# First batch of an attention and MLP kernel stacked on 128 partitions, with fp32 products in column tiles, on one Trainium2 core

## Chip, cores and metric

The kernel runs on one core of a Trainium2 chip. The metric is device time in microseconds (us). Three runs of the kernel before took 362.1, 361.82 and 361.71 us; the median is 361.82.

A core has these engines, named as the profile names them: PE (TensorE, matrix products; PEld are its weight loads), DVE (VectorE), ACT (ScalarE), POOL (GpSimd) and SP (only issues transfers). Each has an instruction queue of its own and takes it in order. Transfers (DMAs) are issued by SP, ACT or POOL and run on 16 shared DMA engines; only those issued by POOL convert the data type on the way. Products land in PSUM, eight banks of 128 partitions x 512 fp32 values.

## Reference

```python
kv  = einsum('bhsd,bhse->bhde', k, v)              # b = 8, h = 8, s = 576, d = 64
out = einsum('bhsd,bhde->bhse', q, kv)
x   = out / sqrt(mean(out*out, -1) + 1e-6) * g_norm    # heads side by side: [8, 576, 512]
a1  = alpha1 * x + beta1
tok = einsum('ts,bsd->btd', w_tok, a1)             # w_tok 576 x 576
u   = x + lam * tok
a2  = alpha2 * u + beta2
out = u + lam * (relu(a2 @ w_ch1) @ w_ch2)         # 512 -> 2048 -> 512
```

All inputs and the output are fp32.

## The kernel before

The eight batches run one after the other. For each there are two parts. The first, of small "fill" products, makes kv = k^T v per head, turns q so that d lies on the partitions, multiplies both, norms the result (`norm_ops`) and mixes tokens with W_tok (`tok`), which gives u in `xm`; then u is scaled and turned into `a2m`. The second part, the "main" stream, is the two big products: ch1 (L1020, 16 blocks of 4 products of 512 columns, then relu on ACT) and ch2 (L1049). The tokens 512 to 575 of two batches share a tail tile.

Nothing is issued in the order in which it is written. `P.op`, `P.dma` and `P.mm` only record operations with a cost, and `schedule()` plays them through: each engine takes the first operation of its list that is ready by the planner's clock, and PE weaves fills between the main products. Before the main stream begins, PE is given idlers (L558, a bf16 product of ones) wherever nothing is ready, and one idler between the products of a slow fill. `P.shift`, a table by operation number, moves single operations in the lists. The order found so is emitted as fixed instruction lists with semaphore waits.

The prologue, all that comes before the main stream, handles batch 0 in four pairs of heads, p = 0 to 3:
- SP loads k, q and v of each pair (`load_early` and L587) on 96 partitions, six tokens each (rows of 1536 bytes), and after the second pair the matrix W_tok, in fp32 (L592, L594).
- k is rounded to fp32r (a shortened fp32 for PE) by POOL (`round_early`, L682), v by ACT (L1144) or POOL (L1148).
- POOL copies q (L693), PE transposes it 96x96 in fp32 (L699), ACT copies it to `qt` (`qt_early`).
- `kv_early` makes k^T v of a pair as six 128x128 fp32r products (L736), of which DVE and ACT keep the two 64x64 blocks on the diagonal (`kvc`).
- `norm_pair` (L868) and `norm_tail` (L887) multiply qt by kvc; per 512 columns `norm_ops` needs ACT (square), DVE (reduce), ACT (root), DVE (reciprocal, scale, multiply to `rm`), then ACT copies x out and POOL multiplies it by g (L839, L841).
- `wt_group` transposes W_tok in fp32 on PE (L1099, L1102), ACT writes it as bf16 to `wt`; `wsums` (L1121, L1123) adds its columns.
- The rows alpha1 lam g and beta1 lam are computed on one partition by DVE, in ten steps, and spread by PE in three bf16 parts (`e1_rows`, L662).
- `tok_pair` mixes the tokens of one pair (L933, 80 products of 128 columns in all), DVE adds (L941), `a2_pair` transposes u (L972) and ACT scales it to `a2m` (L976).

PSUM tiles of the prologue come from banks 1 to 7.

Batch 1 uses the same early path: k and q by SP in fp32 on 96 partitions, k rounded by DVE (L685), v by a casting load on POOL. Batch 2 takes k and v by casting loads (`load_kv`, `kv`, L760 and L766) but its q still by the early path: SP, POOL copy, PE transposes L699. From batch 3 on q is loaded in 32-wide pieces (`load_q`), transposed by DVE (`qt_steady`, L1223), and u is turned by POOL (scale and add, L1004, L1007) and a transposing DMA (`a2_dma`); batches 0 to 2 use `a2_pair`. The weights w1 and w2 are cast by loads on POOL in blocks of 512 (L1190, L1196).

Of the kernel before, what the change touches and what calls it, by code (L numbers as in the profile page):

```python
# [7 lines left out]
F32 = mybir.dt.float32  # L8
# [16 lines left out]
class Op:  # L25


    __slots__ = ("q", "kind", "cost", "lat", "fns", "pri", "idx", "deps", "raw", "alloc",
# [25 lines left out]
class Prog:  # L54
    ENGINES = ("PE", "ACT", "DVE", "POOL")

    def __init__(self, nc, stack):
        self.nc, self.stack = nc, stack
        self.ops, self.lastw, self.readers = [], {}, {}
        self.ps = stack.enter_context(nc.psum_tensor("ps", [128, 8, 512], F32))  # L60
        self.eng = {"PE": nc.tensor, "ACT": nc.scalar, "DVE": nc.vector,
                    "POOL": nc.gpsimd, "SP": nc.sync}
        self.spares = 0
        self.pools = {"main": (0, 1, 2, 3), "fill": (4, 5, 6, 7), "any": tuple(range(1, 8))}
        self.main, self.fill = [], []
# [3 lines left out]
        self.goal, self.last, self.shift = 0, None, {}  # L69
# [35 lines left out]
    def op(self, q, cost, fn, r=(), w=(), pri=0.0, lat=0.15, after=()):  # L105
        o = Op(q, "c", cost, lat, [fn], self.bias + pri, len(self.ops))
        return self._add(o, r, w, after)

    def dma(self, q, slot, nbytes, fn, r=(), w=(), pri=0.0, after=(), issue=0.55):
        o = Op(q, "d", issue, 0.0, [fn], self.bias + pri, len(self.ops))  # L110
        o.slot, o.nbytes = slot, nbytes
        return self._add(o, r, w, after)

    def mm(self, stream, cols, fns, r=(), w=(), slow=False, after=(), margin=0.3,
# [4 lines left out]
        o = Op("PE", "w" if slow and slow != "k" else "m", n * (max(per, {"r": 0.213, "k": 0.25}.get(slow, 0.109)) if slow else max(per, 0.056)),  # L119
               0.24, fns, self.bias, len(self.ops))  # L120
        o.margin, o.narrow, o.urgent = 0.0 if urgent else margin, cols < 512, urgent
# [4 lines left out]
    def schedule(self):  # L126
        far, stack = {}, [(self.main[self.goal], 0.0)]
        while stack:
            o, d = stack.pop()
            if far.get(o, -1.0) >= d:  # L130
                continue
            far[o] = d
            d += o.cost + o.lat + (2.5 if o.kind == "d" else 0.0)
            stack.extend((y, d) for y in o.deps)
        for o in self.ops:
            if o in far:
                far[o] += self.shift.get(o.idx, 0.0)
                if o.kind != "d":
                    o.pri = -self.lead - far[o]
        self.fill.sort(key=lambda o: -far[o] if o in far else 1.0)  # L140
# [314 lines left out]
def bass_transnormer_attn__then__resmlp_affine_kernel(  # L455
# [15 lines left out]
    with ExitStack() as stack:  # L471
# [5 lines left out]
        ident = sb("ident", [128, 128], F32)  # L477
        pick = sb("pick", [128, 128], BF16)
# [39 lines left out]
        def f32(t, letters):  # L518
            return t[0:96].rearrange("p %s -> p (%s)" % (letters, letters)).bitcast(F32)
        k0s = six(f32(w2, "j f")[:, 0:3072])  # L520
        k1s = [t[0:96].rearrange("p c f -> p (c f)")[:, 0:1536].rearrange(
            "p (h c d) -> p h c d", h=4, c=6) for t in (xm[:, 1], tmp)]

        def sk(b, h0, h1):
            if b == 0:
                return k0s[:, h0:h1]
            return k1s[h0 // 4][:, h0 % 4:(h1 - 1) % 4 + 1]
        sq_ = six(xm[0:96, 2:4].rearrange("p b c f -> p (b c f)")[:, 0:3072])
        sv = six(qs[0:96])
        hf = hh[:].bitcast(F32)  # L530
        wl = hf[:, 0:2304].rearrange("p (c s) -> p c s", c=4)
        wlt = hf[0:64, 2304:2880]
# [3 lines left out]
        kr6 = kr[0:96].rearrange("p (r c f) -> p r c f", r=4, c=6)  # L536
        vr6 = six(vr[0:96])
# [14 lines left out]
        def dcost(n, ns):  # L552
# [12 lines left out]
            pattern=[[-1, 128]], channel_multiplier=1), r=["ident"], w=["ident"])  # L565


        def load_v(b, h0, h1, after=(), pri=0.0):
            P.dma("POOL", "v%d_%d" % (b, h0), dcost(96 * (h1 - h0), 105), lambda e: e.dma_start(
                vr6[:, h0:h1].rearrange("p h c d -> p h (c d)"),  # L570
                v[b, h0:h1].rearrange("h (p c) d -> p h (c d)", c=6)),
                w=[("v", p) for p in range(h0 // 2, h1 // 2)], after=after, issue=0.8, pri=pri)

        def load_early(b, h0, h1, what, after=()):
            for n, x in what:
                st = sk(b, h0, h1) if n == "k" else sq_[:, h0:h1]
                P.dma("SP", "%s%d_%d" % (n, b, h0), dcost(96 * (h1 - h0), 80),
                      lambda e, x=x, st=st: e.dma_start(
                          st.rearrange("p h c d -> p h (c d)"),
                          x[b, h0:h1].rearrange("h (p c) d -> p h (c d)", c=6)),  # L580
                      w=[("st", n + "1" * (n == "k" and b), p)
                         for p in range(h0 // 2, h1 // 2)],
                      after=after)

        for p in range(4):
            load_early(0, 2 * p, 2 * p + 2, (("k", k), ("q", q)))
            P.dma("SP", "v0_%d" % p, dcost(96 * 2, 80), lambda e, p=p: e.dma_start(  # L587
                sv[:, 2 * p:2 * p + 2].rearrange("p h c d -> p h (c d)"),
                v[0, 2 * p:2 * p + 2].rearrange("h (p c) d -> p h (c d)", c=6)),
                w=[("sv", p)])  # L590
            if p == 1:
                P.dma("SP", "wl", dcost(512, 130), lambda e: e.dma_start(  # L592
                    wl, moe_w_tok[0:512, :].rearrange("(c p) s -> p c s", p=128)), w=["wl"])
                P.dma("SP", "wlt", dcost(64, 130), lambda e: e.dma_start(  # L594
                    wlt, moe_w_tok[512:576, :]), w=["wlt"])
        P.dma("ACT", "row4", 0.1, lambda e: e.dma_start(rows[0:1, 4, 0:DH], g_norm[None, :]),
              w=[("row", 4)], issue=0.3)
        for i, x in enumerate((moe_alpha1, moe_lam, moe_beta1)):
            P.dma("ACT", "row%d" % i, 0.2, lambda e, i=i, x=x: e.dma_start(
                rows[0:1, i, :], x[None, :]), w=[("row", i)], issue=0.3)  # L600
        for i, x in enumerate((moe_alpha2, moe_beta2)):
# [9 lines left out]
        P.op("DVE", dve(512), lambda e: e.memset(vr[96:128, 2048:2560].bitcast(F32), 0.0),  # L611
             w=["vtz"])
# [7 lines left out]
        def row(i, n=DM):  # L620
            return rows[0:1, i, 0:n]
        lbrow = rows[0:1, 3, :].bitcast(BF16)[:, 0:DM]
        P.bias = -500.0
        P.op("DVE", 0.67, lambda e: e.tensor_tensor(
            out=row(0), in0=row(0), in1=row(1), op=ALU.mult), r=[("row", 0), ("row", 1)],
            w=[("row", 0)])
        x = P.op("DVE", 0.67, lambda e: e.tensor_tensor(
            out=lbrow, in0=row(2), in1=row(1), op=ALU.mult), r=[("row", 1), ("row", 2)],
            w=[("row", 3)])
        P.op("DVE", 0.2, lambda e: e.tensor_scalar(  # L630
            out=row(1, DH), in0=row(4, DH), scalar1=8.0, scalar2=None, op0=ALU.mult),
            r=[("row", 4)], w=[("row", 1)], after=[x])
        P.op("DVE", 0.67, lambda e: e.tensor_tensor(
            out=row(0).rearrange("p (h d) -> p h d", h=NH),
            in0=row(0).rearrange("p (h d) -> p h d", h=NH),
            in1=rows[0:1, 1, None, 0:DH].to_broadcast([1, NH, DH]), op=ALU.mult),
            r=[("row", 1), ("row", 0)], w=[("row", 0)])
        eg = rows.rearrange("p i f -> p (i f)")[:, 0:DM + DH]
        parts = [rows[0:1, i, :].bitcast(BF16)[:, 0:DM + DH] for i in (5, 4, 2)]
        x = None  # L640
        for out_, in_, j, key in ((0, None, 0, ("row", 5)), (None, 0, 0, ("row", 0)),
                                  (1, None, 1, ("row", 4)), (2, 1, 1, ("row", 2))):
            dst = eg if out_ is None else parts[out_]
            after = [x] if x else []
            if in_ is None:
                x = P.op("DVE", dve(576), lambda e, dst=dst: e.tensor_copy(out=dst, in_=eg),
                         r=[("row", 0), ("row", 1)], w=[key], after=after)
            else:
                x = P.op("DVE", dve(576), lambda e, dst=dst, in_=in_: e.tensor_tensor(
                    out=dst, in0=eg, in1=parts[in_], op=ALU.subtract),  # L650
                    r=[("row", 0), ("row", 1), ("row", (5, 4)[in_])],
                    w=[key, ("row", 1)] if out_ is None else [key], after=after)
# [5 lines left out]

        def e1_rows(after):
            for o, n, dst, key in ((0, DM, e1_bc, "e1"), (DM, DH, g_bc, "g")):  # L660
                t = P.bank("any")
# [702 lines left out]
```

## Time and profile before

| what | value |
|---|---|
| runs | 362.1, 361.82, 361.71 us |
| span of the profiled execution (first to last instruction) | 361.3 us |
| its own whole time | not among the three runs |
| DVE, ACT, POOL busy | 194.0, 160.3, 145.2 us |
| idlers L558 | 213, 28.6 us busy |
| ch1 L1020 + ch2 L1049 | 122.3 + 133.1 us busy |
| first ch1 product | 40.79 us |
| DMA | 47.60 MB, mean 132 GB/s |

The profiled span lies 0.5 us below the median run. A line of the list of groups reads: source line, engine, operation, output <- inputs, partitions x elements, count | busy us, mean ns of one | idle time just before, and what ended it. A line of a timeline reads: start, duration, engine, line, operation, count, and in brackets the idle time before it with the engine that ended it. The durations of matmuls overlap, as they are pipelined; the distance from one start to the next is what one costs. A line of the transfers reads: output <- input, the queue, count, KB each (as written), us from issue to landing.

The shares of the first stretches (length, then busy us and instructions of PE, PEld, DVE, ACT and POOL, granted clock, DMA share, GB/s) show where the prologue is dense:

```profile
0.00:10.00 10.00, 6.54 (x49) 6.14 (x50) 6.25 (x14) 3.01 (x5) 3.73 (x10) 1.00 0.84 204
10.00:20.00 10.00, 10.00 (x99) 8.78 (x98) 6.49 (x15) 5.70 (x15) 2.97 (x5) 1.00 1.08 266
20.00:30.00 10.00, 9.94 (x109) 8.69 (x108) 4.08 (x11) 7.25 (x18) 7.71 (x9) 1.00 1.12 229
30.00:40.00 10.00, 10.00 (x163) 9.85 (x162) 7.01 (x14) 5.25 (x12) 8.02 (x10) 1.00 1.25 245
```

### The profile page before, as it was taken

To read this page: it belongs to the slowest core of one execution; us is meant where nothing else is said; L and a number is where in the kernel's file an instruction comes from. 1 tells how busy PE (TensorE), PEld (TensorE's weight loads), DVE (VectorE), ACT (ScalarE), POOL (GpSimd) and SP (SyncE) were. 2 spreads that over 40 slices of the span, in tenths; PEclk is the share of its full clock that TensorE was granted. 3 is DMA by queue.
4 is the path that set the end of the run, shared out by engine and by line. 5 is a ranking of instruction groups with operands and counts; after the bars stand their busy time and mean duration, and the time that the engine had idled before them with its cause. 6 is when DMAs were issued, how large, how long until landed. Compare 5 with 4: busy or idle time off the path is not lost.

```text
span 361.3 us, 5731 instructions
## 1 busy us (share of the span) xinstructions
PE 351.3 (97%) x2308; PEld 211.6 (59%) x2343; DVE 194.0 (54%) x351; ACT 160.3 (44%) x317; POOL 145.2 (40%) x140
## 2 busy tenths in 40 slices
PE   6999999999999999999999999999999999999995
PEld 5989775447576565455466545564475544444644
DVE  6647735772198479528931686258803883210043
ACT  3575467118782177514841356134741273016400
POOL 3269703080306120894077322972372217740000
PEclk9999999999999999999999999999999999999999
DMA  8999999993943990299329940699020210310012
GB/s 196 274 223 245 232 211 284 227 138 121 230 33 99 267 158 17 44 143 308 90 47 149 284 119 0 110 195 280 2 58 33 85 31 15 87 64 24 2 61 85
DMA packets 94578, 47.60 MB, mean 132 GB/s; under 512 B 66829, under 2 KB 89109, under 8 KB 94552
## 3 DMA queue, kind: packets, MB, share of 16 engines
q1 hardware_dynamic: 70704, 27.70, 37.7%
q0 software_dynamic: 23824, 19.53, 31.6%
q8 instruction: 18, 0.29, 0.4%
q14 instruction: 8, 0.07, 0.1%
q10 hardware_dynamic: 24, 0.01, 0.0%
HBM read 38.82 MB, written 9.44 MB: 134 GB/s over the span
## 4 chain that ended last, share of the span: by engine, by line
PE 84%; DMA 11%; POOL 2%; ACT 1%; issue 1%; DVE 0%; SPq 0%
PE ps L1049 30%; PE ps L1020 27%; PE ps L918 8%; DMA w<-in_moe_w_ch_dram 6%; DMA xm<-in_q_dram 5%; PE ps L1032 4%; PE ps L558 2%; PE ps L853 2%; PE ps L760 2%; PE ps L699 2%; PE ps L952 1%; PE ps L972 1%; PE ps L1060 1%; PE ps L736 1%; PE ps L1099 1%
## 5 line engine op out<-in xcount | busy, mean ns | idle before, releaser
L1049 PE MATMUL ps<-w,hh 128*128 128x512 bf16 x541 | 133.1, 382 | 0.6
L1020 PE MATMUL ps<-a2m,w 128*128 128x512 bf16 x497 | 122.3, 381 | 0.6 <-issue 0.2
L1015 ACT ACTIVATE hh<-ps 128x512 bf16<-128x512 f32 x144 | 85.2, 597 | 84.0 <-PE ps L1020 74.9
L1049 PEld LDWEIGHTS ps<-w,hh 128*128 128x128 bf16 x560 | 52.9, 98 | 57.2 <-issue 0.8
L1020 PEld LDWEIGHTS ps<-a2m,w 128*128 128x128 bf16 x512 | 48.9, 98 | 53.4 <-issue 0.4
L1076 DVE TENSOR_TENSOR tmp<-ps,lam_bc 128x512 f32<-128x512 f32 (+2 forms) x38 | 25.1, 663 | 73.2 <-PE ps L1049 71.0
L1081 POOL TENSOR_TENSOR xm<-xm,tmp 128x512 f32<-128x512 f32 x28 | 35.4, 1272 | 57.3 <-DVE tmp L1076 57.3
L1004 POOL TENSOR_TENSOR a1f<-xm,a_bc 128x512 f32<-128x512 f32 x20 | 25.3, 1272 | 55.4 <-DVE xm L925 55.2
L853 PE MATMUL ps<-kvc,qt 128*128 128x128 f32 x140 | 42.3, 410 | 0.0
L821 DVE TENSOR_REDUCE small<-sq 128x8 f32<-128x512 f32 (+2 forms) x41 | 26.9, 663 | 22.6 <-ACT sq L818 22.5
L818 ACT ACTIVATE sq<-ps 128x512 f32<-128x512 f32 (+2 forms) x41 | 23.9, 583 | 34.0 <-PE ps L853 32.9
L558 PE MATMUL ps<-fil 128*128 128x128 bf16 x213 | 28.6, 246 | 3.4 <-DVE fil L557 3.4
L925 DVE TENSOR_TENSOR xm<-ps,xm 128x512 f32<-128x512 f32 x28 | 19.3, 689 | 22.5 <-PE ps L918 22.4
L1007 POOL TENSOR_TENSOR a2b<-a1f,b_bc 128x512 bf16<-128x512 f32 x23 | 28.9, 1271 | 0.3
L853 PEld LDWEIGHTS ps<-kvc,qt 128*128 128x128 f32 x140 | 28.0, 200 | 1.5
L918 PE MATMUL ps<-rm,wt 128*128 128x512 bf16 x112 | 28.7, 379 | 0.0
L760 PE MATMUL ps<-vr,kr 128*128 128x128 f32 x96 | 28.1, 397 | 0.0
L829 DVE TENSOR_TENSOR ps<-ps,small 128x512 f32<-128x512 f32 (+2 forms) x41 | 27.3, 677 | 0.6
L833 DVE TENSOR_TENSOR rm<-ps,e_bc 128x512 bf16<-128x512 f32 x32 | 21.4, 674 | 0.6 <-ACT e_bc L666 0.4
L558 PEld LDWEIGHTS ps<-fil 128*128 128x128 bf16 x213 | 19.0, 113 | 3.8 <-DVE fil L557 3.4
L760 PEld LDWEIGHTS ps<-vr,kr 128*128 128x128 f32 x96 | 18.5, 199 | 1.3
L1223 DVE STREAM_TRANSPOSE qp<-qs 128x576 f32<-128x576 f32 x20 | 15.0, 761 | 6.4 <-PE ps L699 5.8
(108 smaller groups left out, 358.7 us busy)
## 6 DMA issues: line engine op xcount, KB each, us to landing
out_dram<-xm SPq DMA_DIRECT2D x32, 256.0 KB, 3.2
kr<-in_k_dram POOLq DMA_DIRECT2D x6, 1024.0 KB, 7.6
vr<-in_v_dram POOLq DMA_DIRECT2D x6, 1024.0 KB, 10.6
qs<-in_q_dram SPq DMA_DIRECT2D x20, 288.0 KB, 4.7
w<-in_moe_w_ch_dram POOLq DMA_DIRECT2D x8, 512.0 KB, 15.4
xm<-in_q_dram SPq DMA_DIRECT2D x4, 576.0 KB, 12.8
w<-in_k_dram SPq DMA_DIRECT2D x4, 288.0 KB, 8.5
xm<-in_q_dram SPq DMA_DIRECT2D x4, 288.0 KB, 9.2
```

Source lines behind the costliest of these rows:

```text
L558: P.spare_fn = lambda e: e.matmul(P.ps[:, 0, 0:128], fil[:], fil[:], start=True, stop=True)
L760: P.mm("fill", 128, [lambda e, t=t, c=c, h=h, o=128 * (h % 4): e.matmul(t.ap()[:, o:o + 128], kr4[:, h, c:c + 2, :].rearrange("p c d -> p ...
L821: P.op("DVE", dve(n), lambda e: e.tensor_reduce(out=st, in_=sq[rs, s3, 0:nst, :], axis=AX.X, op=ALU.add), r=[("sq", s3)], w=[("sm", s4)])
L829: P.op("DVE", dve(n), lambda e: e.tensor_tensor(out=grp(ps()), in0=grp(ps()), in1=st[..., None].to_broadcast([rs.stop - rs.start, nst, DH] ...
L853: P.mm("fill", 128, [lambda e, p=p: e.matmul(dst(p), qt[:, p, cs], kvc[:, i, p, :], start=(p == 0), stop=(p == 3)) for p in range(4)], r=[ ...
L918: P.mm("fill", 512, [lambda e, sc=sc: e.matmul(t.ap(), wt[:, sc if sc < 4 else tw(b), 128 * c:128 * c + 128], rsrc(b, sc, al), start=(sc = ...
L1004: P.op("POOL", pool(512), lambda e: e.tensor_tensor(out=a1f[:, s], in0=x, in1=a2_bc[:], op=ALU.mult), r=ks + ["a2"], w=[("a1f", s)])
L1007: y = P.op("POOL", pool(512), lambda e: e.tensor_tensor(out=a2b[:, c], in0=a1f[:, s], in1=b2_bc[:], op=ALU.add), r=[("a1f", s), "b2"], w=[ ...
L1015: P.op("ACT", act(512), lambda e: e.activation(dst, t.ap(), ACT.Relu), r=[t], w=keys, pri=-1000)
L1020: P.mm("main", 512, [lambda e, dj=dj: e.matmul(t.ap(), w1[:, dj, 128 * fj:128 * fj + 128], a2m[:, b % 3, dj, :], start=(dj == 0), stop=(dj ...
L1049: P.mm("main", 512, [lambda e, fj=fj, t=t, c=c: e.matmul(t.ap(), (ht[:, fj, 128 * c:128 * c + 128] if c < 4 else hl[:, fj, :]), w2[:, fj, ...
L1081: lambda e: e.tensor_tensor(out=x, in0=x, in1=tmp[:, s, a:z], op=ALU.add),
```

## The change

Batch 0 is handled in two halves of four heads, j = 0 and 1, instead of four pairs.
- `load_pair` loads k, q and v of a pair on 128 partitions (two heads of 64 groups of nine tokens, rows of 2304 bytes), in the order k0 q0 q1 k1 v0 v1 q2 q3 k2 k3 v2 v3.
- `qt_first` turns q without rounding or copying: plain fp32 products with the identity as the moving operand, 64 output rows each, one pair in the lower and one in the upper half of the columns (36 products of 128 columns). ACT writes `qt`.
- `kv_first` makes k^T v from the loaded fp32 values in 64x64 tiles, 72 products of 64 columns, the two row halves alternating and writing different banks. The roundings of k and v (round_early, L1144, L1148) go.
- `norm_half` and `tok_half` take two column blocks of four heads; tok has 40 products of 256 columns.
- W_tok comes as bf16 by casting loads on POOL, after v of pair 1 has landed; its transposes are bf16.
- alpha1, lam and g are loaded by ACT onto all 128 partitions, after the first k; DVE multiplies them in place. `e1_rows` goes, and so does the later load of lam on SP.
- Batch 1: k and v by `load_kv` (casting loads), kv by `kv`; q still early. Batch 2: q by `load_q` and `qt_steady`, u by `a2_dma`. So `qt_early` runs for batch 1 alone and `a2_pair` for batches 0 and 1.
- w1 and w2 are loaded in blocks of 512, 1024, 512 and of 1024, 1024.
- The planner works back from due times, with another start time and a long table of shifts and extra ordering (`P.gate`).

In the instruction order that results, 361 products stand before the first ch1 product (before: 419), 141 of them idlers (213), and 1880 from it on (1924). POOL's queue begins: W_tok, the first w1 block, W_tok's last 64 rows, v and the tails of k and v of batch 1, then the multiplies of `norm_half` with two w1 loads, k of batch 1 and half of w2 between them. PE's begins: 12 products of `qt_first`, 36 of `kv_first`, 24 of `qt_first` with 10 of `norm_half`, 18 of `kv_first`, four W_tok transposes, 18 of `kv_first`, the other W_tok transposes and `norm_half` of j = 1. The idlers' operand is set as the last of nine DVE operations at the start, and no idler stands ahead of the first products.

```diff
-        for p in range(4):
-            load_early(0, 2 * p, 2 * p + 2, (("k", k), ("q", q)))
...
+            P.dma("SP", "%s0_%d" % (n, p), dcost(128, 100), lambda e: e.dma_start(
+                dst[:, p].rearrange("p c d -> p (c d)"),
+                x[0, 2 * p:2 * p + 2].rearrange("h (g c) d -> (h g) (c d)", c=9)),
+                w=[("st", n, p)])
...
+        wgate = [P.lastw[("st", "v", 1)][0]]
+        P.dma("POOL", "wl", dcost(512, 90), lambda e: e.dma_start(
+            wl, moe_w_tok[0:512, :].rearrange("(c p) s -> p c s", p=128)), w=["wl"],
+            after=wgate, issue=0.9)
...
+        def qt_first(j):
+            banks = [P.bank("any") for _ in range(3)]
+            for i, t in enumerate(banks):
+                for m in range(2):
+                    P.mm("fill", 128, [lambda e, c=c, t=t, m=m, i=i: e.matmul(
+                        t.ap(slice(64 * m, 64 * m + 64))[
+                            :, 128 * (c - 4 * i):128 * (c - 4 * i) + 128],
+                        q0s[:, 2 * j + m, c, :], ident[:], start=True, stop=True,
+                        tile_position=(0, 64 * m))
+                        for c in range(4 * i, min(4 * i + 4, 9))],
+                        r=["ident", ("st", "q", 2 * j + m)], w=[t], slow=0.2, urgent=True)
...
+        def kv_first(j):
+            ts = [P.bank("any") for _ in range(2)]
+            for m in range(2):
+                p = 2 * j + m
+                P.mm("fill", 64, [lambda e, c=c, s=s, t=t, m=m, p=p: e.matmul(
+                    t.ap(slice(64 * m, 64 * m + 64))[:, 0:64],
+                    k0s[64 * s:64 * s + 64, p, c, :], sv[64 * s:64 * s + 64, p, c, :],
+                    start=(c == 0), stop=(c == 8), tile_position=(64 * s, 64 * m))
+                    for c in range(9) for s, t in enumerate(ts)],
+                    r=[("st", "k", p), ("st", "v", p)], w=ts, slow=0.11, urgent=True)
...
         def mix(b):
...
-                if b > 2:
+                if b > 1:
                     a2_dma(b, c)
-            if b < 3:
+            if b < 2:
                 for p in range(4):
                     a2_pair(b, p)
...
+        P.t0 = 41.7
+        P.pace = 1.28
+        P.shift = {
...
+        P.gate = {
```

More of the change, by code (lines that the diff above doesn't have):

```diff
@@ L596, in bass_transnormer_attn__then__resmlp_affine_kernel @@
[L596 to L600, printed above, removed]
+        P.op("DVE", dve(128), lambda e: e.tensor_copy(out=identb[:], in_=ident[:]),
+             r=["ident"], w=["identb"])
+        lo, up = slice(0, 64), slice(64, 128)
@@ new lines, in bass_transnormer_attn__then__resmlp_affine_kernel @@
+        P.dma("POOL", "wlt", dcost(64, 90), lambda e: e.dma_start(
+            wlt, moe_w_tok[512:576, :]), w=["wlt"], after=wgate, issue=0.7)
+        for x, dst, key, n in ((moe_alpha1, e1_bc, "e1", DM), (moe_lam, lam_bc, "lam", DM),
+                               (g_norm, g_bc, "g", DH)):
+            P.dma("ACT", key, dcost(128, 86 if n == DM else 30), lambda e, x=x, dst=dst, n=n: e.dma_start(
+                dst[:], x[None, :].to_broadcast([128, n])), w=[key], issue=0.4,
+                after=[P.lastw[("st", "k", 0)][0]])
@@ L601, in bass_transnormer_attn__then__resmlp_affine_kernel @@
+        P.dma("ACT", "row", 0.1, lambda e: e.dma_start(rows[0:1, 2, :], moe_beta1[None, :]),
+              w=[("row", 2)], issue=0.3)
         for i, x in enumerate((moe_alpha2, moe_beta2)):
@@ L630, in bass_transnormer_attn__then__resmlp_affine_kernel @@
[L630 to L652, printed above, removed]
+        P.op("DVE", 0.2, lambda e: e.tensor_scalar(
+            out=g_bc[:], in0=g_bc[:], scalar1=8.0, scalar2=None, op0=ALU.mult), r=["g"],
+            w=["g"])
@@ L1218, in load_kv @@
                     tl[0:64], x[b, :, 512:576, :].rearrange("h s d -> s h d")),
-                    w=[n + "t"], issue=0.8)
+                    w=[n + "t"], issue=0.8, after=after)
         def qt_steady(p):
```

468 lines of the change are left out of this document (203 added, 265 removed), and 44 rows, old and new, of the table cs.

## Prediction

> **What bounds the kernel now.** I read the page's busy shares first, then TensorE's (PE's) own waits, then PE's timeline where its waits and its stream begin, then the DMA issues.
>
> ```profile
> PE 351.3 (97%) x2308; PEld 211.6 (59%) x2343; DVE 194.0 (54%) x351; ACT 160.3 (44%) x317; POOL 145.2 (40%) x140
> ...
> PE ps L558 <- DVE fil L557: 3.4, 1, 3.4
> PE ps L699 <- POOL qp L693: 0.7, 1, 0.7
> PE ps L1020 <- issue: 0.2, 1, 0.2
> ```
>
> PE is busy 351.3 of 361.3 us, and of its 10.0 us of idle 3.4 stand before the first matmul, 0.7 in one wait, some 4.5 behind the last one. So the end is set by a sum: the moment at which the main stream starts, plus all PE work behind it.
>
> ```profile
> 3.38 2.74 PE L558 MATMUL ps<-fil 128*128 128x128 bf16 x24 [3.38 <-DVE fil L557]
> ...
> 30.62 2.46 PE L558 MATMUL ps<-fil 128*128 128x128 bf16 x41
> ...
> 40.79 1.24 PE L1020 MATMUL ps<-a2m,w 128*128 128x512 bf16 x5
> ...
> 73.20 0.71 PE L699 MATMUL ps<-ident,qp 96*128 96x96 f32 x6 [0.68 <-POOL qp L693]
> ...
> 81.59 1.97 PE L972 MATMUL ps<-ident,xm 128*128 128x128 f32 x16
> 83.39 0.60 PE L983 MATMUL ps<-ident,xt 128*128 128x128 f32 x4
> ```
>
> The main stream starts at 40.79; 320.5 us follow it. Before 40.79 PE shows busy, but 213 of its products there are idlers (L558) that only keep it going, so that stretch is a chain of loads, products and norms.
>
> **Behind the start: what PE loses.** The built order of the changed kernel has 1880 matmuls from the first ch1 matmul on, against 1924. Three kinds go; nothing is added.
> - 24 transposes of batch 2's q (its q now comes by load_q and DVE transposes). Their four groups hold PE from 73.20 to 73.75, 74.62 to 75.33, 84.73 to 85.64 and 88.32 to 88.81: 2.66 us.
> - With them goes the wait of 0.68 us at 73.20. What is late next there is token mixing of batch 1, whose input is on the chip.
> - 16 transposes of batch 2's x (a2_pair, now a2_dma): 81.59 to 83.39, 1.80 us.
> - Batch 1's k^T v takes 20 instead of 24 products: the 24 of L736 stand from 47.82 to 53.57 with 15 ch1 matmuls of 0.216 between them, so (5.75 - 3.24)/24 = 0.105 each; 4 x 0.105 = 0.42.
>
> Sum 5.6 us. What replaces them lies off PE: 8 POOL passes of 1.27 us (rows L1004 and L1007), 4 DMA transposes, 4 DVE transposes of 0.76 (L1223), all for batch 2, whose ch1 is needed only after batches 0 and 1, some 80 us later. I cost them at nothing; without that cover it would be POOL's 10 us. SP's q loads for batch 2 wait for the second half of w2, as late as before.
>
> **Before the start: the new prologue.** Loads first.
>
> ```profile
> w<-in_k_dram SPq DMA_DIRECT2D x1, 288.0 KB, 3.5
> ...
> qs<-in_v_dram SPq DMA_DIRECT2D x1, 288.0 KB, 7.2
> ...
> hh<-in_moe_w_tok_dram SPq DMA_DIRECT2D x1, 1152.0 KB, 10.3
> ...
> w<-in_moe_w_ch_dram POOLq DMA_DIRECT2D x1, 512.0 KB, 14.2
> ...
> vr<-in_v_dram POOLq DMA_DIRECT2D x1, 1152.0 KB, 18.4
> ```
>
> Each is one issue, with KB and us to landing; issue times from SP's timeline. k0 lands at 0.74 + 3.5 = 4.2 and v1, the sixth, at 3.22 + 7.2 = 10.4: 1.24 us a load, in runs of 1536 bytes. W_tok, in runs of 2304, lands 1296 KB between 10.4 and 14.8: 295 KB a us. The changed loads have runs of 2304, so 0.98 us each: q0 at 5.2, v1 at 4.2 + 5 x 0.98 = 9.1, plus 1.8 for the 544 KB of broadcast rows that ACT now loads: 10.9. q2 and q3 follow by 12.9, then k2, v2, k3, v3 beside POOL's W_tok load; SP kept some 170 KB a us beside such loads (k and q of batch 1, 2304 KB from 23.2 to 36.8), so v3 lands near 19.7 (before: 23.2).
>
> W_tok now waits for v1 and goes out on POOL as a casting load. Bounds for it: 10.3 us from issue, as on SP, gives 10.9 + 10.3 = 21.2; the 18.4 of the 1152 KB casting load of v gives 29.3. The first w1 load's 14.2 for 1024 KB read, scaled to 1152, gives 26.9; by the rate (two w1 loads, 2 MB, from 22 to 37.5) it would be 22.1. I take 24.
>
> PE second. The 36 products that transpose q and the 72 of k^T v in 64x64 tiles are full fp32 matmuls, which no row shows. Bounds for 128 columns: 0.119 (L760, the rounded fp32, 8 in 0.95) from below; from above a second doubling, since rounded fp32 already takes twice the 0.056 of bf16 (L933, 5 in 0.28): 0.24. I take 0.22, near the upper end, as unrounded operands should not be cheaper than rounded ones; with 64 columns half, 0.11.
>
> A cold PE takes double: the 24 idlers at 3.38 took 0.114 each, the 41 at 30.62 only 0.056, the change falling at 11.8, 8.4 us after the first. That early stream was sparse until 9.85, and the dense run from there was 2 us long. The new stream starts at 5.3 and is dense: warm between 7.3 and 13.7; I take 10.6.
> By the Trainium skill (TensorE: Matmul & The Clock Gate, Part 1) the clock rises after about 3.4 us of sustained work; the 8.4 us here disagree unless a sparse stream doesn't count. By the rule alone the start would be about 1 us earlier, by 8.4 us about 1.5 later.
>
> So: 12 cold q products 5.3 to 10.6; 36 of k^T v, 4.0, to 14.6; 24 q products, 5.3, to 19.9; 10 attention products (0.13, from L868) with 6 idlers, 1.7, to 21.6; 18 of k^T v, 2.0, to 23.6. Now the queue stands at the first W_tok transposes until 24, and behind them wait the last 18 of k^T v: 26.3 with both. From there to the main stream the order holds 135 idlers x 0.056 = 7.6; 40 token products of 256 columns at half of 0.216, 4.3; 16 transposes of x at 0.116, 1.9; 10 attention products 1.3; column sums of W_tok 1.4; 21 bf16 transposes 1.7 (0.056 to 0.115 each, I take 0.08); one of 8 columns 0.2: 18.3 in all. The DVE chain in it (two pairs' norms at once: reduce, scale and multiply of 2 x 512 and 256 columns, 7.5 us with W_tok's rows) ends just before PE asks for it. Main start 26.3 + 18.3 = 44.6, against 40.79: 3.8 later. Before, the last k^T v ended at 26.7, so its tail took 14.1; the new one is longer because half of all heads, not a quarter, is normed behind the last product.
>
> POOL's and DVE's old work (rounding k and v, copying q, the row arithmetic) goes; none of it ended last but L693.
>
> **The sum.** 361.3 + 3.8 - 5.6 = 359.5 of span. The median run is 361.82, 0.5 above the span; the profiled run's own time isn't among the three, so I add 0.5: **360.0 us**.
>
> **Rivals.**
> - Row tiles run at once. The two row halves alternate in k^T v and write different banks, so they may overlap: 0.055 each. Then 36 end at 12.6, PE is at W_tok by about 20.6, and W_tok bounds. With it at 22.1, start 22.4 + 1.0 + 18.3 = 41.7: 357.1. Against it: column halves and accumulation in one stream. The Trainium skill (TensorEngine Tiling, Key Properties) says that different tiles load and multiply in parallel; no row here shows it.
> - Slower: W_tok lands late. PE is in order, so each us past 23.6 moves the end by one, through 18 products of k^T v. At 26.9 the time is 362.9, at 29.3 it is 365.3; from 26.5 it decides for slower. For it: both casting rows, 14.2 and 18.4. Against it: their queue held several loads.
> - The tail waits. The old tail held about 1 us of waits beyond its instructions, and POOL's multiplies stand behind two loads' waits; 1 to 2.5 us more: 361.0 to 362.5, no change.
> - Batch 1's k lands late. It now stands on POOL's queue behind 2 MB of w1 and is wanted at 44.6 + 4; at 3 to 4 us a MB it lands near 46. Two or more us late: 362 and up.
> - The change doesn't free PE: excluded for the 44 matmuls by the order.
>
> **Chances.** Forecast 0.45 (359.0 to 361.1), tiles at once 0.17, W_tok late 0.20, waiting tail 0.10, batch 1 late 0.08. What a measurement can tell from no change here is about 0.2%, so faster is below 361.1, slower above 362.5: faster 0.59 (most of the first and all of the second), same 0.17, slower 0.24. Range 357.0 to 363.5: it takes in the second case whole and the third up to W_tok at 27.5; what lies past that, and the worse half of a late batch 1, is about 0.15.
>
> **What would show it.** First ch1 matmul at 44 to 45.5; from it to the end 315; no L699-like group for batch 2 and no wait near 73; k^T v tiles paced 0.11, q products 0.22; W_tok's transposes starting near 24. The forecast is wrong if the start lies below 42 or above 47, or if PE stands idle behind it.

## The result and the profile after

The changed kernel takes 373.95 us (median of four runs, 373.38 to 374.69), the kernel before beside it 361.76: a ratio of 1.0334 with a 95% interval of 1.0306 to 1.0363. The forecast was 360.0 us, range 357.0 to 363.5, with 0.24 for slower. The profiled execution took 373.97 us, its span is 372.1. Comparisons leave disturbed executions out, among them the two longest of experiment 5 and the profiled one of experiment 9.

Line numbers from here on are those of the changed kernel: L676 q products of batch 0 (`qt_first`), L719 its k^T v (`kv_first`) and L730 the copies of that on DVE, L855 its attention products (`norm_half`), L1084 the W_tok transposes, L834 attention and L760, L762 the k^T v copies of later batches, L1002 ch1, L986, L989 and L993 the two passes and the DMA of `a2_dma`.

The page of the kernel after, busy shares, granted clock in 40 slices and the lines of the chain that ended last:

```profile
PE 352.2 (95%) x2349; PEld 208.1 (56%) x2349; DVE 189.0 (51%) x348; ACT 156.2 (42%) x303; POOL 143.9 (39%) x136
...
PEclk9959999999999997999999999999999999999998
...
PE ps L1031 31%; PE ps L1002 31%; PE ps L900 8%; PE ps L1014 4%; DMA a2m<-a2b 3%; DMA g_bc<-in_g_norm_dram 3%; PE ps L576 2%; PE ps L834 2%; PE ps L743 2%; PE ps L934 1%; DMA w<-in_k_dram 1%; PE ps L915 1%; PE ps L719 1%; PE ps L855 1%; PE ps L954 1%; PE ps L1042 1%
```

PE is busy 352.2 us, as before (351.3), though the built order has fewer products (2241 against 2343; the page counts a plain fp32 product twice): some ran slowly. The clock row shows where: the third slice (18.6 to 27.9 us) stands at 5 tenths, and a slice near 140 at 7. Two transfers stand in the chain with 3% each that were not in it before, a2m<-a2b and g_bc<-in_g_norm_dram. PE's waits (engine, line, releaser: sum, count, longest):

```profile
PE ps L855 <- DVE kvc L730: 4.8, 1, 4.8
PE ps L1002 <- DMA a2m<-a2b: 4.8, 1, 4.8
PE ps L676 <- DMA xm<-in_q_dram: 4.4, 1, 4.4
PE ps L834 <- DVE kvc L762: 1.4, 1, 1.4
```

Of these four only the first q product (L676, the wait for the first load) was in the forecast. The wait at L855 stands in the prologue, the one at L1002 ahead of batch 2's ch1.

**First loss: 14.4 to 28.7 us.** PE's timeline of the prologue, and the windows between its turning points (PE, PEld, DVE, ACT, POOL busy, then granted clock, DMA share, GB/s):

```profile
4.42 4.33 PE L676 MATMUL ps<-ident,xm 128*64 128x128 f32 x24 [4.42 <-DMA xm<-in_q_dram]
8.68 2.14 PE L719 MATMUL ps<-qs,w 64*64 64x64 f32 x72
10.75 3.66 PE L676 MATMUL ps<-ident,xm 128*64 128x128 f32 x44
19.24 0.44 PE L855 MATMUL ps<-kvc,qt 128*128 128x128 f32 x1 [4.83 <-DVE kvc L730]
...
47.30 1.46 PE L1002 MATMUL ps<-a2m,w 128*128 128x512 bf16 x6
```

```profile
10.75:14.40 3.65, 3.65 (x48) 3.42 (x44) 0.00 (x0) 2.47 (x5) 1.36 (x2) 1.00 1.03 205
14.40:19.20 4.80, 0.01 (x1) 0.00 (x0) 1.42 (x5) 1.14 (x3) 0.10 (x1) 0.94 1.10 186
19.20:28.70 9.50, 9.46 (x97) 7.96 (x97) 5.54 (x12) 3.25 (x8) 0.69 (x1) 0.50 1.50 254
```

The loads were early and the products cheap: PE had its q products done at 14.41, where the forecast had 19.9. Then it stood for 4.83 us, and the products behind that ran at a granted clock of 0.50 for 9.5 us. DVE's timeline shows what it waited for:

```profile
17.72 0.20 DVE L642 TENSOR_SCALAR g_bc<-g_bc 128x64 f32<-128x64 f32 x1 [13.05 <-DMA g_bc<-in_g_norm_dram]
17.93 0.23 DVE L730 CAST kvc<-ps 64x64 fp32r<-64x64 f32 x1
18.17 0.68 DVE L652 TENSOR_TENSOR a2m<-a2m,lam_bc 1x512 bf16<-1x512 f32 x1
18.88 0.22 DVE L730 CAST kvc<-ps 64x64 fp32r<-64x64 f32 x1
```

The copies of k^T v (L730) were ready to be made at about 11, but stand in DVE's queue behind L642, the multiplication of g_bc by 8, and L642 waited 13.05 us for the load of g_bc. That load is 32 KB. ACT issued it at 7.93, third after e1_bc and lam_bc, and it took 9.8 us to land, while the DMA engines were full (share 1.03 and 1.10 in the first two windows). The planner counts 4.2 us from issue for a transfer so small (`o.end = t + (4.2 if t < 20 else 2.6)`), so in its plan the row comes 5.6 us earlier than it did.

**Second loss: 135 to 144 us.** SP's and POOL's queues ahead of batch 2's ch1, and PE there:

```profile
128.29 0.57 SPq L1177 DMA_DIRECT2D qs<-in_q_dram  x1
128.91 2.32 SPq L993 DMA_TRANSPOSE a2m<-a2b  x1
```

```profile
128.95 0.94 POOL L1185 DMA_DIRECT2D kr<-in_k_dram  x1
```

```profile
139.86 10.41 PE L1002 MATMUL ps<-a2m,w 128*128 128x512 bf16 x36 [4.81 <-DMA a2m<-a2b]
```

```profile
139.80:144.00 4.20, 4.14 (x10) 1.49 (x11) 2.91 (x5) 1.11 (x2) 0.00 (x0) 0.50 1.90 264
```

The last of the four DMA transposes that make u of batch 2 was issued at 128.91 and landed 10.9 us later (median of the four: 3.3), 4.81 us after PE wanted it; POOL's load of batch 4's k, the first of 2.25 MB, was issued 0.04 us behind it. PE's 36 products then took 10.41 us instead of 7.93 (experiment 4); the last line, a window, shows the granted clock of 0.50 (until 144.9). POOL's passes had ended at 127.4, so they left the last transpose some 6 us before PE wanted it.

### The profile page after: what moved, and what is told of

It reads as the page before. It is cut to its first block, busy times and chain, and to the rows that moved or that the text cites. A ratio compares the mean times of both kernels' runs of the same rounds, so it can differ in the third digit from the quotient of the medians.

```text
span 372.1 us, 5753 instructions
## 1 busy us (share of the span) xinstructions
PE 352.2 (95%) x2349; PEld 208.1 (56%) x2349; DVE 189.0 (51%) x348; ACT 156.2 (42%) x303; POOL 143.9 (39%) x136
## 4 chain that ended last, share of the span: by engine, by line
PE 90%; DMA 7%; DVE 1%; SPq 0%; POOL 0%; ACTq 0%; issue 0%; ACT 0%
PE ps L1031 31%; PE ps L1002 31%; PE ps L900 8%; PE ps L1014 4%; DMA a2m<-a2b 3%; DMA g_bc<-in_g_norm_dram 3%; PE ps L576 2%; PE ps L834 2%; PE ps L743 2%; PE ps L934 1%; DMA w<-in_k_dram 1%; PE ps L915 1%; PE ps L719 1%; PE ps L855 1%; PE ps L954 1%; PE ps L1042 1%
## 5 line engine op out<-in xcount | busy, mean ns | idle before, releaser
L1031 PE MATMUL ps<-w,hh 128*128 128x512 bf16 x560 | 136.8, 382 | 0.0
L1002 PE MATMUL ps<-a2m,w 128*128 128x512 bf16 x512 | 123.5, 387 | 4.8 <-DMA a2m<-a2b 4.8
L1002 PEld LDWEIGHTS ps<-a2m,w 128*128 128x128 bf16 x512 | 49.3, 99 | 61.6 <-DMA a2m<-a2b 5.3
L986 POOL TENSOR_TENSOR a1f<-xm,a_bc 128x512 f32<-128x512 f32 x24 | 30.3, 1270 | 88.7 <-DVE xm L907 88.6
L834 PE MATMUL ps<-kvc,qt 128*128 128x128 f32 x140 | 40.1, 396 | 1.4 <-DVE kvc L762 1.4
L989 POOL TENSOR_TENSOR a2b<-a1f,b_bc 128x512 bf16<-128x512 f32 x27 | 34.0, 1273 | 0.4
L907 DVE TENSOR_TENSOR xm<-ps,xm 128x512 f32<-128x512 f32 x28 | 19.4, 692 | 28.4 <-PE ps L900 28.4
L743 PE MATMUL ps<-vr,kr 128*128 128x128 f32 x112 | 31.9, 397 | 0.0
L900 PE MATMUL ps<-rm,wt 128*128 128x512 bf16 x112 | 28.7, 379 | 0.0
L834 PEld LDWEIGHTS ps<-kvc,qt 128*128 128x128 f32 x140 | 26.8, 199 | 3.3 <-DVE kvc L762 1.5
L743 PEld LDWEIGHTS ps<-vr,kr 128*128 128x128 f32 x112 | 21.8, 200 | 0.8
L1195 DVE STREAM_TRANSPOSE qp<-qs 128x576 f32<-128x576 f32 x24 | 17.9, 761 | 7.6 <-ACT qt L1198 4.4
L1198 ACT ACTIVATE qt<-qp 128x576 fp32r<-128x576 f32 x24 | 16.1, 680 | 7.6 <-DVE qp L1195 7.5
L760 ACT ACTIVATE kvo<-ps 64x256 f32<-64x256 f32 x14 | 5.3, 379 | 32.8 <-PE ps L749 32.6
(99 smaller groups left out, 320.5 us busy)
```

The costliest lines, as they stand in the source:

```text
L743: P.mm("fill", 128, [lambda e, t=t, c=c, h=h, o=128 * (h % 4): e.matmul(t.ap()[:, o:o + 128], kr4[:, h, c:c + 2, :].rearrange("p c d -> p ...
L834: P.mm("fill", 128, [lambda e, p=p: e.matmul(dst(p), qt[:, p, cs], kvc[:, i, p, :], start=(p == 0), stop=(p == 3)) for p in range(4)], r=[ ...
L900: P.mm("fill", 512, [lambda e, sc=sc: e.matmul(t.ap(), wt[:, sc if sc < 4 else tw(b), 128 * c:128 * c + 128], rsrc(b, sc, al), start=(sc = ...
L986: P.op("POOL", pool(512), lambda e: e.tensor_tensor(out=a1f[:, s], in0=x, in1=a2_bc[:], op=ALU.mult), r=ks + ["a2"], w=[("a1f", s)])
L989: y = P.op("POOL", pool(512), lambda e: e.tensor_tensor(out=a2b[:, c], in0=a1f[:, s], in1=b2_bc[:], op=ALU.add), r=[("a1f", s), "b2"], w=[ ...
L1002: P.mm("main", 512, [lambda e, dj=dj: e.matmul(t.ap(), w1[:, dj, 128 * fj:128 * fj + 128], a2m[:, b % 3, dj, :], start=(dj == 0), stop=(dj ...
```

## Experiments

All start from the changed kernel. Its planned order is kept, and single operations are moved in it after planning (experiment 7 reorders the products of one line instead): `behind(i, j)` puts operation i right behind operation j; every engine takes its own operations in the order that results. Ratios are against the kernel before on the same chip.

**1. DVE's copies ahead of the rows.** 32 is L642, 35 is L652, 53 the second copy L730.

```diff
         P.schedule()
...
+        for x in (35, 32):
+            behind(x, 53)
         P.synchronize()
```

> Changed kernel, every load as it is; on DVE alone the two copies of k^T v of pairs 0 and 1 (L730) stand ahead of the multiplication of g_bc (L642) and of the lam row (L652). Theory (DVE's queue stands 13.05 us behind the load of g_bc, and PE's 4.83 us before L855 are owed to the copies queued behind it; PE, idle so long, then runs at a granted clock of 0.50 until 28.7): the wait before L855 goes, the products behind it take half, W_tok (landed by about 20) is the next to be late; the main stream starts near 40 instead of 47.30 and the time is 365.5 to 368. Rival 1 (the copies are not what PE waits for): nothing changes, 374. Rival 2 (the norms' chain on DVE and ACT, which needs e1_bc and lam_bc, sets the main stream's start anyway): start 43 to 47, time 370 to 374.

Measured: 365.94 us, ratio 1.0110 [1.0061, 1.0158]; main stream from 40.91. PE's waits:

```profile
PE ps L1002 <- DMA a2m<-a2b: 3.2, 1, 3.2
...
PE ps L1084 <- DMA hh<-in_moe_w_tok_dram: 0.9, 1, 0.9
```

The wait at L855 is gone, the clock is 1.00 throughout the prologue, and W_tok is next to be late (0.9). So the copies' place in DVE's queue cost 47.30 - 40.91 = 6.4 us, and rivals 1 and 2 fall. The load of g_bc itself was not touched. The rest of the gain of 8.9 us of span is the second loss, here 3.2 instead of 4.8 and without half clock behind it, less 1.7 that a new stretch of half clock cost: it stands from 50.0 to 53.4, behind a wait of 1.36 us at L834 that the changed kernel has too, there without half clock behind it.

**2. The gap filled with idlers.** 55 is the first L855; each `P.idler(2)` is two idlers.

```diff
+        spot = at(55)
+        P.sequence[spot:spot] = [(P.idler(2),) for _ in range(40)]
```

> Changed kernel with 80 more idlers on PE (L576, 0.056 each, 4.5 us) just ahead of L855 of pairs 0 and 1, where PE stood idle from 14.41 to 19.24; the wait itself stays. Theory (the idle time costs twice: once as itself, once because the granted clock stood at 0.50 for the 9.4 us behind it): L855 still starts near 19.2, k^T v of pair 2 takes 1.1 instead of 2.19, the main stream starts 4 to 4.7 earlier, near 43, time 369.3 to 370. Rival (the stretch behind is bound by DVE's and ACT's norms or by W_tok, not by PE): the same start within 1, time 373 to 374.

Measured: 365.08 us, ratio 1.0068 [1.0030, 1.0105]; span of the profiled execution 362.8, main stream from 43.82. The windows of the first loss again:

```profile
14.40:19.20 4.80, 4.80 (x83) 4.47 (x80) 1.23 (x4) 1.37 (x3) 0.81 (x1) 1.00 1.16 192
19.20:28.70 9.50, 8.90 (x143) 7.67 (x143) 7.24 (x18) 5.88 (x16) 1.37 (x2) 1.00 1.39 269
```

L855 starts at 19.44 as before, the clock stays at 1.00, and the start is 3.5 us earlier than 47.30: the price of the half clock alone. The expected time was missed by 4 us on the good side because the second loss vanished too, which the expectation did not foresee; its reason shows below.

**3. u of batch 2 by PE again.** The eight POOL passes and four DMA transposes of batch 2 are replaced by 16 PE transposes and four ACT scalings between ch2's products; all other orders stay.

```diff
+        gone = {P.ops[j + 5 * x] for j in (421, 422, 423) for x in range(4)}
+        P.sequence = [u for u in P.sequence if u[0] not in gone]
...
+            m2 = P.mm("fill", 128, [lambda e, c=c, pp=pp, tb=tb: e.transpose(
+                tb.ap()[:, 128 * c:128 * c + 128], xm[:, 2, c, 128 * pp:128 * pp + 128],
+                ident[:]) for c in range(4)],
...
+            a2 = P.op("ACT", 0.6, lambda e, pp=pp, tb=tb: e.activation(
+                a2m[:, 2, pp, :], tb.ap(), ACT.Identity, bias=b2c[:, pp:pp + 1],
...
```

> Changed kernel, but u of batch 2 is made as in the kernel before: 16 transposes on PE and 4 scalings on ACT behind L749, in place of 8 passes on POOL and 4 DMA transposes; everything else in the same order. Theory (the forecast's cover of 80 us was misread: u of batch 2 can begin only when its token mixing ends near 120, 15 us ahead of its first layer, and POOL, SP and the DMA queues take longer than that): the 4.81 us wait at 135 and the cold stretch behind it (36 products in 10.41 instead of 7.8) go, 1.8 of transposes come back: time 374 - 4.8 - 2.6 + 1.8 = 368.4, range 367.5 to 369.5. Rival (PE would be late there anyway, through ACT's or the banks' waits): 371 to 374.

Measured: 367.83 us, ratio 1.0165 [1.0126, 1.0204]. PE waits for nothing at L1002; 36 products take 7.93. As expected; 0.9 of a new wait (L834 behind ACT's last scaling) is in it.

**4. The loads wait for the transposes.** 544 to 547 are POOL's loads of batch 4's k and v, 551 the last q load, 438 the last transpose. Nothing else moves.

```diff
+        for x in (544, 545, 546, 547, 551):
+            P.ops[x].deps.add(P.ops[438])
```

> Changed kernel, u of batch 2 by DMA transposes as it is; the four loads of batch 4's k and v on POOL and the last q load on SP wait until the last of the four transposes has landed. Theory of contention (the last transpose, issued at 128.91, takes 10.9 us against a median of 3.3 because 2.25 MB of k and v start with it): it lands by 133, PE's wait of 4.81 goes with its cold stretch, time 374 - 7.4 = 366.6, range 366 to 368. Rival (the passes on POOL and SP's queue, with the q loads and stores ahead of the transpose, are what is late): it lands at 137 or later, the wait is 2 us or more, time 370 to 374.

Measured: 365.66 us, ratio 1.0102 [1.0066, 1.0138], span 364.1. POOL's first load of batch 4 shows when the last transpose, issued at 128.08, landed, and PE's waits hold no L1002:

```profile
132.32 0.94 POOL L1185 DMA_DIRECT2D kr<-in_k_dram  x1 [3.90 <-DMA a2m<-a2b]
```

```profile
PE ps L855 <- DVE kvc L730: 5.1, 1, 5.1
PE ps L676 <- DMA xm<-in_q_dram: 4.4, 1, 4.4
PE ps L834 <- DVE kvc L762: 1.4, 1, 1.4
```

It landed after 4.0 us, and the time is a little below the expected 366 to 368. Contention it is; POOL's passes and SP's queue are in time. Seven runs give the same from another side, since the lead of the last transpose over POOL's k load differed by chance: -0.09 us (experiment 7) and 0.04 (the changed kernel): 10.9 us to landing; 0.10, 0.14 and 0.16 (experiments 8, 6 and 1): 9.7, 9.7, 9.4; 0.87 (experiment 2): 5.4; with the loads held back: 4.0 (3.8 to 4.3 in experiments 5, 10 and 11). That is why the second loss vanished in experiment 2. The changed kernel itself shows it once more, where PE does not wait: the last transpose of batch 4, issued at 208.30 with POOL's first load at 208.16, took 9.4 us. The Trainium skill (DMA: Bandwidth & Descriptors, Queues, rings and completion order) says that each DMA engine takes turns between queues packet by packet; the leads agree, as far as they go: a transpose that is not done when the casting loads begin would share with them to its end.

**5. Experiments 1 and 4 together.**

> Changed kernel with both edits that worked alone: DVE's two copies of k^T v ahead of the multiplication of g_bc, and the loads of batch 4's k and v and the last q load behind the landing of batch 2's last DMA transpose. Theory (the two losses are separate and add up): main stream from 40.9 as with the first edit alone, the wait of 3.15 at 130 gone, no cold stretch: span 363.2 - 3.15 = 360.0, time near 361.9, level with the kernel before (its 362.05 on this chip) within 0.3%. Rival (the transposes are late even so, now that all of it comes 6 us sooner, or the delayed k and v of batch 4 are late for their products): a wait of 2 us or more stays, time 364 or more.

Measured: ratio 1.0010 [0.9981, 1.0038]. The spans of its twelve executions run from 358.3 to 364.6, and the longer ones have the lower mean granted clock (1.000 for the shortest, 0.979 for the two longest); the profiled one took 362.9. There no wait stands at L1002 of batch 2, but the main stream starts at 44.07 instead of 40.9: waits of 0.3, 0.5, 0.7 and 1.2 us between 15 and 25 (ACT's copies of q, W_tok, ACT's and DVE's copies), and then a granted clock of 0.50 from 26.7 to 30.1. A second such stretch, from 54.0 to 57.4, follows the wait at L834. In experiment 1 waits of 0.3, 0.9 and 0.8 left the clock of the prologue at 1.00. The median says that the two losses add up as expected. That the half clock makes the spread is argued from the mean clocks, since only one execution has a profile.

**6. g first of the three rows.** 20 is the load of e1_bc, 22 that of g_bc.

```diff
+        u = P.sequence.pop(at(22))
+        P.sequence.insert(at(20), u)
```

> Changed kernel, only ACT's three broadcast loads in another order: g, e1, lam instead of e1, lam, g, all at the same gate; DVE's order is as it is, with the lam row (L652) between the two copies of k^T v. Theory (DVE is held by whichever load its next instruction in order needs; g's 9.8 us are those of the third load of a queue beside 400 GB/s of others, not its own): g lands 2 us or more earlier, L642 runs by 15, but L652 now stands for lam, which lands no earlier than g did: PE's wait is 4 to 5.5 us as before, time 373 to 375. Rival (g alone is what is late): the wait falls below 2, time 368 or less.

Measured: 371.35 us, ratio 1.0264 [1.0230, 1.0298]. DVE's timeline:

```profile
12.98 0.20 DVE L642 TENSOR_SCALAR g_bc<-g_bc 128x64 f32<-128x64 f32 x1 [8.31 <-DMA g_bc<-in_g_norm_dram]
...
17.25 0.68 DVE L652 TENSOR_TENSOR a2m<-a2m,lam_bc 1x512 bf16<-1x512 f32 x1 [3.83 <-DMA lam_bc<-in_moe_lam_dram]
17.96 0.22 DVE L730 CAST kvc<-ps 64x64 fp32r<-64x64 f32 x1
```

g_bc now lands 5.7 us after issue and L642 runs at 12.98, but the second copy stands behind L652, which waits for lam_bc until 17.25. PE's wait is 3.70 and the time 371.35, each a little under what was expected (4 to 5.5, and 373 to 375). The wait has in the main only changed its name: what has to move is the queue's order, not one load.

**7. One row half after the other.**

```diff
-                    for c in range(9) for s, t in enumerate(ts)],
+                    for s, t in enumerate(ts) for c in range(9)],
```

> Changed kernel; in the 64x64 products of k^T v of batch 0 the nine of one row half stand behind one another, and then the nine of the other, instead of alternating; the same 72 products. If two row tiles overlap (the rival of the prediction, 0.059 a product measured), the 36 of pairs 0 and 1 take about twice the 2.14 us, near 4.2, 0.117 each; if the product simply costs 0.06, they take 2.1 again.

Measured: span 377.1, a single run. PE's timeline, to be read against the 8.68 line above; each fp32 product shows as two records, so x72 are 36 products:

```profile
9.10 4.05 PE L719 MATMUL ps<-qs,w 64*64 64x64 f32 x72
```

4.05 us instead of 2.14, 0.1125 instead of 0.059 a product: row tiles that alternate overlap almost whole, and without that the forecast's 0.11 is right. This agrees with the Trainium skill (TensorEngine Tiling, Key Properties), by which different tiles work in parallel. The two row halves write different banks, so both change with the order, and the run doesn't tell which of them the overlap needs.

**8. The rows at the very start.** ACT issues g, lam and e1 first of all, without their wait for the first k.

```diff
+        for x in (22, 21, 20):
+            P.ops[x].deps.clear()
+            P.ops[x].raw.clear()
+            P.sequence.insert(at(23), P.sequence.pop(at(x)))
```

> Changed kernel; ACT issues the three broadcast loads (g, lam, e1; 544 KB) at the very start, with no wait for the first k; DVE's order is as it is. Theory (only the landing matters): all three land by about 9, DVE's wait ends before the first products of k^T v do, PE's wait before L855 goes; the first q pair comes 1 to 2 us later, so the main stream starts at 41.5 to 43, time 367 to 369 with the loss at 135 left in it. Rival (the loads of q, k and v lose as much as DVE gains): first q product at 7 or later, start 44 or later, time 370 or more.

Measured: 368.87 us, ratio 1.0193 [1.0157, 1.0229]; g lands after 4.6 us, L642 runs at 5.37, PE does not wait at L855; but the first q product starts at 6.37 instead of 4.42 and the main stream at 41.98. As expected: 544 KB ahead of q cost 1.95 us, about the 1.8 that the forecast charged for them.

**9 to 11. A version that beats both.** First 24 idlers at the short waits of experiment 5 (88, 85 and 94 are W_tok transposes):

```diff
+        for x, pairs in ((88, 4), (85, 3), (94, 5)):
+            spot = at(x)
+            P.sequence[spot:spot] = [(P.idler(2),) for _ in range(pairs)]
```

> Both edits together (copies first; loads wait), and 24 idlers more on PE where it stood idle in short waits between 19 and 25: 8 ahead of the first transpose of W_tok, 6 ahead of its third group, 10 ahead of its fourth. Theory (the two edits alone varied from 358.3 to 362.9 of span because about 2.4 us of short waits there let the granted clock fall to 0.50 near 27 in some executions and not in others): the clock stays at 1.00 to the main stream, which starts at 40 to 41; span 40.5 + 317.4 (what followed the start where only the loads waited) = 358 to 359, time 360 to 361 with less spread, faster than the kernel before by 0.2 to 0.6%. Rival (the spread is that of the loads): starts from 40 to 44 and times from 360 to 364 as before.

Measured: ratio 1.0002 [0.9977, 1.0027], spans 358.8 to 361.8: a little less spread, but not faster; the expected 360 to 361 was missed, and without a usable profile it stays open why.

> The same with one unit of four ch1 products of batch 0 (L1002) moved from behind the first eight attention products of batch 1 (L834) to ahead of them, where PE waited 1.36 us for DVE's L762. Theory (that wait is a plain hole in PE's order that work at hand can fill): the wait falls from 1.36 to about 0.5, and the time is 0.9 below the kernel without this edit, 359 to 360.5. Rival (what comes behind needs those eight products by then): the same time as without it.

The edit: `u = P.sequence.pop(at(302))`, then `P.sequence.insert(at(231), u)`. Measured: 361.71 us, ratio 0.9993 [0.9963, 1.0024]; the expected 359 to 360.5 was missed. The wait at L834 is gone, but another took its place, with half clock behind it (products of 0.65 instead of 0.39 us):

```profile
51.20 1.04 PE L1002 MATMUL ps<-a2m,w 128*128 128x512 bf16 x4 [1.77 <-DMA w<-in_moe_w_ch_dram]
```

That is the second quarter of w1: POOL issued it at 37.16 behind k of batch 1 and half of w2, and it took 14 us. With the prologue 6 us shorter, PE gets there first. So, last, on POOL's queue (172 is that load, 180 the first half of w2):

```diff
+        P.sequence.insert(at(180), P.sequence.pop(at(172)))
```

> The last kernel (copies first, loads wait, 24 idlers, ch1 unit ahead) with the load of the second quarter of w1 (L1162, 512 KB, issued at 37.16, landed at 51.2) moved on POOL's queue ahead of the first half of w2 (L1168, issued at 34.99). Theory (with the prologue's wait gone the next to be late is this load: PE waited 1.77 us for it and then ran at half clock for some 3.5 us): it lands near 48, PE waits for nothing there, span 361.2 - 1.8 - 1.7 = 357.7 to 358.5, time near 360, faster than the kernel before by 0.4 to 0.8%. Rival (the queues' total traffic sets its landing, not its place): it still lands at 51 and the time stays at 361.7.

Measured: 360.93 us (360.3 to 362.08), ratio 0.9961 [0.9943, 0.9979]; span of the profiled execution 358.4, as expected. The load, issued at 35.10, lands after 10.6 us, ahead of the 48 expected. Busy shares, then the longest of PE's waits:

```profile
PE 346.0 (97%) x2337; PEld 205.4 (57%) x2373; DVE 188.4 (53%) x348; ACT 155.5 (43%) x303; POOL 144.0 (40%) x136
```

```profile
PE ps L676 <- DMA xm<-in_q_dram: 4.5, 1, 4.5
PE ps L1084 <- DMA hh<-in_moe_w_tok_dram: 0.7, 1, 0.7
```

Behind the first product no wait over 0.7 is left, and the mean granted clock is 0.998. This is the only version that is faster than the kernel before, by 0.4 per cent.

## Why the prediction was wrong

By its own sum the span was to be 359.5; it is 372.1, 12.6 more: 2.7 ahead of the main stream (44.6 forecast, 47.30 measured) and 9.9 behind it (314.9 forecast, 372.1 - 47.3 = 324.8 measured). Two steps failed, one on each side.

- **The step that failed behind the start: "I cost them at nothing", for u of batch 2 by POOL and DMA, "some 80 us" ahead of need.** The 16 transposes at 81.59, which the forecast took for batch 2's, are those of batch 1 (they still stand in the kernel after, at 81.89). In the kernel before, batch 2's stand from 125.72 to 128.3 and its ch1 begins at 131.59:

```profile
125.72 1.47 PE L972 MATMUL ps<-ident,xm 128*128 128x128 f32 x12
...
131.59 0.39 PE L1020 MATMUL ps<-a2m,w 128*128 128x512 bf16 x1
```

  So u is ready for turning only when token mixing of batch 2 ends (119.41 in the kernel after), 15 us ahead of ch1. The price of 1.80 was right, the place was not, and with the place went the cover. It cost 4.81 of idle and 2.5 of half clock; experiments 3 and 4 take both away. What decided within those 15 us was contention of the last transpose with 2.25 MB of loads, not POOL's 10 us, which the forecast named as the price without cover: its passes took until 127.4, some 8 of the 15 us, and were in time.
- **The step that failed ahead of the start: ACT's row loads.** They were charged 1.8 us of bandwidth (experiment 8: 1.95), and nobody was asked who waits for them. DVE's in-order queue did, and behind it PE: 4.83 idle, and half clock to 28.8 (6.4 us of start, experiment 1).
- **The start.** Its 2.7 us hide larger errors of both signs. Up to the last q product: 14.41 instead of 19.9, 5.5 early (first q at 4.42 instead of 5.3, cold q products 4.3 instead of 5.3, k^T v 2.1 instead of 4.0, q products 0.166 instead of 0.22). Then 4.83 of waiting. From there to the end of k^T v 9.45 instead of 6.4, at half clock. The tail: 18.6 instead of 18.3, right.
- **The prices of products.** 0.11 held only without overlap (experiment 7: 0.1125), and 0.22 was 0.166. The rival "row tiles run at once" had the mechanism (0.055 forecast, 0.059 measured) and, with the wait gone, the start: 41.7 forecast, 40.91 in experiment 1.
- **W_tok.** Taken at 24, bounds 21.2 to 29.3; experiment 1, in which PE waits for it, shows 19.94, outside them: issued at 9.02 on POOL, 10.9 us, near SP's 10.3. The 22.1 "by the rate" does not follow from the figures beside it: 2048 KB from 22 to 37.5 are 132 KB a us, so 1152 KB from 10.9 would land at 19.6. The rival "W_tok lands late" was wrong.
- **Cold clock.** Double price ended no later than 8.7, where k^T v begins at full speed: 4.3 us after the first product, not the 8.4 that the old sparse stream had shown. It varies: in experiment 3 the first 36 products of k^T v took 2.83 instead of 2.14, which puts the end some 5.9 us after the first product. The Trainium skill's 3.4 us (TensorE: Matmul & The Clock Gate, Part 1) lies nearer to both than 8.4.
- **PE's saving behind the start.** 5.6 forecast. With the second loss removed (experiment 4) start to end takes 364.1 - 46.7 = 317.4, against 320.5 before: 3.1 saved. 1.36 of the rest is the new wait at L834; 1.1 is not explained, and single executions of the kernel before differ by more (spans of 358.9 to 363.7). With 4.81 and 2.5 for the second loss these 2.5 make up the 9.9.
- **Rivals "waiting tail" and "batch 1's k late".** Neither happened in the changed kernel: the tail took 18.6, and L743 waited for no load. With the first loss gone (experiment 1) the tail took 19.4, 0.8 of it a wait.

The forecast's sign was wrong because no rival held a transfer that busy DMA engines make late: the row behind which DVE's queue stood, and the last transpose. What it named as proof against itself did show: PE idle behind the start, and a start above 47.

## What to carry to other kernels

When a change adds loads, ask for each of them which engine has the first instruction that needs it, and what stands behind that instruction in the engine's order: here 32 KB held PE for 4.8 us through two copies that had nothing to do with it. Before an edit is costed at nothing, find its operation for this very batch in the trace, and measure the time from the moment its input exists to its first use; then list what else is issued to the DMA engines in that time. An idle time of some 5 us on PE is to be charged with half clock behind it as well (2.5 to 3.5 us here); even 1.36 us cost 1.7 more in some runs.

## What was not expected of the hardware

- The granted clock changes in steps of time. In every profile it is 1.00 or 0.50, and counted from a run's first change all others fall on whole multiples of 3.413 us, within 0.01: in the changed kernel 18.60, 28.84, 138.06 and 144.89 are steps 0, 3, 35 and 37. So half clock lasts whole steps: three at the first loss, two at the second, five in experiment 7, though there PE was busy with small fp32 products for nearly all of it.
- The length of the idle time alone does not decide. The same wait of 1.36 us at L834 was followed by one step at 0.50 in experiments 1, 2, 5 and 8, where it fell whole between two multiples, and by none in the changed kernel and experiments 3, 4, 6 and 7, where a multiple cut it in two. The 3.15 us ahead of L1002 in experiment 1, cut too, were followed by none. What rule lies behind it stays open.
- In the first 4 us of the prologue the clock row shows 1.00 while products took twice their later time (12 q products in 4.26 us, 22 in 3.66): at the start the row does not show the slower pace.
- A 128x64 row load (32 KB) took 4.6 us as the very first transfer, 5.7 as the first of three beside loads of q, k and v, and 8.6 to 10.3 as the third.
- Batch 2's DMA transposes of 128x512 bf16 took 2.5 to 5.4 us, and 9.4 to 10.9 when the issue of 2.25 MB of casting loads began within 0.16 us of theirs.
